# Twelve pieces of w_out's combinations: due times for their stores, other steps and other staging places

## The chip, the cores and the metric

One core of one Trainium2 chip runs the whole program. The metric is the device time of one execution in microseconds (us), as the median over runs. The profile is one further execution of the same program, taken with the hardware profiler.

## The reference

The program computes windowed attention followed by a feed-forward layer with squared ReLU, all in float32:

```python
scores = scale * np.matmul(q, k.transpose(0, 1, 3, 2))      # batch 8, 8 heads, 576 positions, head size 64
mask = (rel >= 0) & (rel < 64)                               # rel = query position - key position
attn = softmax(where(mask, scores, -1e9));  attn_out = attn @ v
x = attn_out.transpose(0, 2, 1, 3).reshape(4608, 512)
h = x @ w_in                                                 # 512 x 2048
out = (np.maximum(h, 0.0) ** 2) @ w_out                      # 2048 x 512
```

Only the last product matters for the change: some of `w_out` is not used as it stands, but as sums and differences of its blocks.

## The kernel before

The 4608 tokens are cut in 12 tiles of 384. Every float32 operand of a product is split into a high and a low part, and a product is three matmuls. The first four tiles go the plain way. The other eight are done in four rounds of two tiles, and each round is eight steps, so there are **steps 0 to 31**. A step s belongs to pair p = s mod 8 of 128-column blocks of `w_in`.

In each step TensorE (PE) first makes seven products with combinations of `w_in` (line 932, 7 x 6 matmuls, function `product`), in the manner of Strassen. Their sums leave PSUM by VectorE (DVE, line 949) and ScalarE (ACT). Then PE does the second layer for the step two back (line 1023, function `second`, 3 x 12 matmuls). From step 26 on the second layer is done with combinations of `w_out` (line 1164, function `fast`). In between come the sections of attention of later tiles: scores, softmax, a transposition (line 276) that needs the weights which GpSimd (POOL) has scaled (line 272), and the product with v (line 298).

Before a round starts, its seven operands are made from the two tiles' attention results (function `operands`). Three subtractions (line 884) run on POOL, the first two into the slab `t`; after them ACT rounds (line 895) and DVE takes the rest (line 896). The operands overwrite those of the round before. Rounds begin at steps 0, 8, 16 and 24.

The combinations of `w_out` that steps 26 and later use are made beforehand by `mixing2` (line 1043), in twelve pieces: six pairs p = 0 to 5, each in two halves c. One piece is six POOL instructions (two additions, line 1051, and four subtractions, line 1055), a rounding on ACT (line 1062), a subtraction on DVE (line 1064) and two stores to the DRAM tensor `mixed2` (line 1067; the trace calls this tensor `mixed`, too). The half c = 0 is made in steps 10 to 15 and c = 1 in steps 18 to 23, a pair per step. A piece needs a **staging place** in SBUF: even pairs use the slab `t`, odd pairs the last quarter of the two slabs `gb0` and `gb1` (key "m2"). In `gb` the low part is written over the place in which POOL builds the sums, so the next piece there can begin on POOL only when the second store has been read out. Slab `t` has three separate parts, and it is also the scratch of `operands`.

The order of instructions on each engine comes from a planner (class `Plan`). Every instruction is recorded with an engine, a cost, the keys it reads and writes, and, for transfers, a landing time. `in_order` gives each a latest start, counted back from the PE instruction that needs it (`late[n]`), and then lists the instructions by simulated time, taking among the ready ones the one with the earliest latest start. A store is needed only by what reads the keys it wrote, so without such a reader nearby its latest start is far off. This order is all that the planner gives: each engine runs its list in order, waiting on semaphores where data or space is missing. All transfers are issued by SyncE (SP) from one such list.

Of the kernel before, what the change touches and what calls it, by code (L numbers as in the profile page):

```python
# [8 lines left out]
F32 = mybir.dt.float32  # L9
# [20 lines left out]
def window_attention_relu2_ffn(ctx: ExitStack, tc: tile.TileContext, q, k, v, w_in, w_out, out):  # L30
    nc = tc.nc
    pe, dve, act, pool, sp = nc.tensor, nc.vector, nc.scalar, nc.gpsimd, nc.sync
    B, H, S, D = q.shape
    NT, DM = out.shape
# [19 lines left out]
    raw_t = att.tile([P, 2, 2, S], F32, name="raw")  # L54
# [306 lines left out]
    def slab(name, dtype, words=4 * DM):  # L361
        if name not in slabs:
            slabs[name] = wpool.tile([P, words], dtype, name="w")
        return slabs[name]
# [62 lines left out]
    def in_turn(x):  # L427
        return x.rearrange("p (a b) -> p b a", a=2)
# [32 lines left out]
    E = mybir.EngineType  # L461
# [55 lines left out]
    mixed2 = dram.tile([NF // 2, P, 4, 2, DM // 2], F32, name="mixed2")  # L517
# [29 lines left out]
    with tc.manual_schedule(engines={E.PE, E.DVE, E.Activation, E.Pool, E.SP}):  # L547
        for token in order.split():
            op, eng = token[0], token[-1] if token[-1] in "dap" else None
            n = int(token[1:].rstrip("dap"))  # L550
# [92 lines left out]
    NP = NF // 2  # L643
# [74 lines left out]
    plan = Plan()  # L718

    def by(op, *args):  # L720
        return lambda: op(*args)
# [3 lines left out]
    wi_n, wo_n, wi, wo = [0], [0], {}, {}  # L725

    def wi_fetch(name, source, keys=()):
        n = wi_n[0]
        wi_n[0] += 1
        slot = n % NWI  # L730
        wi[name] = slot
        plan("sp", 0.45, lambda: sp.dma_start(wi_slot(slot).bitcast(F32), source), keys, [("wi", slot)], 3.5,
             freed(wi_home(slot)[0]) if n < NWI else [], 0.7)
# [16 lines left out]
    def wo_keys(slots):  # L750
        return [("wo", slot, m) for slot in slots for m in range(2)]
# [4 lines left out]
    def block(f, half):  # L756
        return kept[f, :, 0, :, half * 2 * P:(half + 1) * 2 * P]
# [160 lines left out]
    def product(s, n):  # L918
        p = s % NP
        kind = (0, "A11", 2, 3, "A12", "A22", 1)[n]  # L920
        source = mixed[p, :, kind] if isinstance(kind, int) else block(2 * p + (kind[1] == "2"), int(kind[2]) - 1)
        wi_fetch((s, n), source, [("mixed", p, c) for c in range(2)] if isinstance(kind, int) else [])
        slot = wi[s, n]
        if n < 4:
            sums_of[s, n] = bank()
        ps, key = sums_of[s, (0, 1, 2, 3, 1, 2, 3)[n]]

        def do():
            w, x, m = wi_slot(slot), operand(n), 0
            for kk in range(2):  # L930
                for part, xx in ((0, 0), (0, 1), (1, 0)):
                    pe.matmul(ps[:, :TT], lhsT=w[:, part, kk * P:(kk + 1) * P], rhs=in_turn(x[:, xx, kk]),  # L932
                              start=n < 4 and m == 0, stop=m == 5, skip_group_check=True)
                    m += 1
        plan("pe", 0.98, do, [("xo", n, 0), ("xo", n, 1), ("wi", slot)], [key, ("tick", s, n)])
        b, a, c, d = (sums_of.get((s, m), (None, None)) for m in range(4))
        sc, v, u = by(short, 0), lambda: r_t[:, s % 2], by(short, 1 + s % 2)
        kv, ku = ("r", s % 2), ("u", s % 2)
        g11, g21 = ((lambda m=m: g_first(s)[:, m], g_first_keys(s, m)) for m in range(2))
        g12, g22 = ((lambda m=m: g_last(s % 4)[:, m], [("gb", s % 4, m)]) for m in range(2))  # L940
        first_a = [("ghi", m) for m in range(3)] + [("glo", m) for m in range(2)] if s < 3 else []
        if LAST <= s < LAST + 4:
            first_a = [("XF", s % 4 // 2, m, r) for m in range(2) for r in range(SPT)]
        squares = SQUARES if s < LAST else LAST_SQUARES
        first_b = freed(f"gb{s % 4 // 2}") if s < 4 else []
        first_s = freed("part1", "t") if s < 2 else []

        def add(to, keys, ps, kps, other, ko, after=()):
            plan("dve", 0.6, lambda: dve.tensor_tensor(to(), ps, other(), ALU.add), [kps, ko], keys, 0, after)  # L949

        def square(g, pre, where):
            x, keys = g
            if where == "dve":
                plan("dve", 0.57, lambda: dve.scalar_tensor_tensor(x(), x(), 0.0, x(), ALU.max, ALU.mult), [], keys)
                return
            if not pre:
                plan("act", 0.5, lambda: act.activation(x(), x(), AF.Relu), [], keys)
            if where == "act":
                plan("act", 0.5, lambda: act.activation(x(), x(), AF.Square), [], keys)
            else:  # L960
                plan("pool", 0.95, lambda: pool.tensor_tensor(x(), x(), x(), ALU.mult), [], keys)  # L961
        if n == 0:
            plan("act", 0.5, lambda: act.copy(sc(), b[0][:, :TT]), [b[1]], ["sc"], 0, first_s)
        elif n == 1:
            add(v, [kv], a[0][:, :TT], a[1], sc, "sc")
        elif n == 2:
            add(u, [ku], c[0][:, :TT], c[1], v, kv, first_s)
        elif n == 3:
            add(lambda: by_half(g22[0]()), g22[1], ordered(d[0][:, :TT]), d[1], lambda: ordered(u()), ku, first_b)
            square(g22, False, squares[0])  # L970
        elif n == 4:
            plan("act", 0.5, lambda: act.activation(by_half(g11[0]()), ordered(a[0][:, :TT]), AF.Relu), [a[1]], g11[1], 0, first_a)  # L972
            square(g11, True, squares[1])
        elif n == 5:
            add(lambda: by_half(g21[0]()), g21[1], ordered(c[0][:, :TT]), c[1], lambda: ordered(v()), kv, first_a)
            square(g21, False, squares[2])
        elif n == 6:
            add(lambda: by_half(g12[0]()), g12[1], ordered(d[0][:, :TT]), d[1], lambda: ordered(v()), kv, first_b)
            square(g12, False, squares[3])
# [55 lines left out]

    def staging(n):
        x, y = (slab(f"gb{m}", F32)[:, 3 * DM:] for m in range(2))
        z = slab("t", F32)  # L1040
        return [z[:, m * DM:(m + 1) * DM] for m in range(3)] if n else [x, y, x]

    def mixing2(op, s, p, c):
        at = lambda m, dtype=F32: staging(1 - p % 2)[m].bitcast(dtype).rearrange("p (f l c) -> p f l c", f=2, l=2)
        mine = ["m2"] if p % 2 else [("T", 0), ("T", 1)]

        def whole(f):
            slot = wo[(s - 2) // NP, 2 * p + f]
            hi, lo = (wo_slot(slot)[:, part].bitcast(F32).rearrange("p (l c) -> p l c", l=2)[:, :, c * P:(c + 1) * P]
                      for part in range(2))  # L1050
            pool.tensor_tensor(at(0)[:, f], hi, lo, ALU.add)

        def less(to, a, b):
            x = at(0)
            pool.tensor_tensor(x[:, to[0], to[1]], x[:, a[0], a[1]], x[:, b[0], b[1]], ALU.subtract)
        if op == "A":
            for f in range(2):
                plan("pool", 0.81, by(whole, f), wo_keys([wo[(s - 2) // NP, 2 * p + f]]) + [("tick", s, 0)], mine)
            for to, a, b in (((0, 0), (0, 1), (0, 0)), ((0, 1), (1, 1), (0, 1)), ((1, 1), (1, 1), (0, 0)), ((1, 0), (1, 1), (1, 0))):
                plan("pool", 0.54, by(less, to, a, b), [], mine)  # L1060
        elif op == "C":
            plan("act", 0.62, lambda: act.copy(at(1, F32R), at(0)), [("tick", s, 6)], mine)
        elif op == "E":
            plan("dve", 0.7, lambda: dve.tensor_tensor(at(2, F32R), at(0), at(1), ALU.subtract), [("tock", s, 0)], mine)
        else:
            for part in range(2):
                plan("sp", 0.5, lambda part=part: sp.dma_start(
                    mixed2[p, :, :, part, c * P:(c + 1) * P], at(1 + part).rearrange("p f l c -> p (f l) c")),
                     mine + [("tick", s + 1, 1)], [("mixed2", p, c, part)], 4.5, (), 0.9)

    FAST = ("A11", 0, 0), ("A12", 1, 0), ("A22", 2, None), ("S1", 0, None), ("S2", 3, None), ("S4", 1, 1), ("S3", 1, None)

# [140 lines left out]
    for n in range(2 * NF + LAG, NPLAIN * NF):  # L1213
        m = n - 2 * NF
# [14 lines left out]
    marks = {}  # L1229
    for j in range(FULL):  # L1230
        for r in range(2 * SPT):
            i = SPT * NPLAIN + 2 * SPT * (j + 1) + r
            m = 16 * j + (2 * r if r else -4)
            m, n = (0, (1, 4)) if m == 2 else (m, m + 1)
            marks.setdefault(m, []).append(by(burst, i, i - 1))
            marks.setdefault(n, []).append(by(cross, i))
    for c in range(2):
        for p in range(NP - 2):
            s = NP * (c + 1) + 2 + p
            for op, at in ("A", (s, 0)), ("C", (s, 6)), ("E", (s, 7)), ("F", (s + 1, 1)):  # L1240
                marks.setdefault(at, []).append(by(mixing2, op, s, p, c))
    operands(0)
    for s in range(NP * FULL + 2):
        if s < NP * FULL:
            for mark in marks.get(2 * s, []):
                mark()
            for n in range(7):
# [3 lines left out]
                if s < LAST and s % 2 == 0 and n % 2 == 0 or s == FAST_END + 1 and n % 2 == 0:  # L1251
                    f = s // 2 * 2 % NP * 2 + n // 2
# [61 lines left out]
```

## Time and profile before

| what | us |
|---|---|
| median of 3 runs | 869.51 (868.71 to 870.89) |
| the profiled execution itself | 869.36 |
| its span, first to last instruction | 867.6 |
| TensorE busy | 835.3 (96%) |
| VectorE busy | 627.6 (72%) |
| ScalarE busy | 435.6 (50%) |
| GpSimd busy | 244.8 (28%) |

A busy share is an average over the span. TensorE is the engine that is nearly always busy, so time is lost where it stands still or where its granted clock is below 1.00; the other engines count where TensorE waits for them. The mean granted clock is 0.986.

### The profile page before, as it was taken

The page shows a single profiled execution, that of the slowest core. Times are in us where ns is not written, and L with a number is a line of the kernel's source. Part 1 is how long each engine was busy: PE and PEld are TensorE (multiplying, and loading weights), DVE is VectorE, ACT ScalarE, POOL GpSimd, SP SyncE. Part 2 cuts the span into 40 slices and gives each one's busy share as a digit, 9 for nine tenths or more (in the row PEclk, how much of TensorE's full clock was granted, in tenths as well). Part 3 has the DMA queues.
Part 4 walks back from the last instruction along what each step waited for, and adds up shares of the span by engine and source line. Part 5 has one row for each costly group of instructions (what it writes and reads, how often), then busy time and mean ns, then how long its engine had stood idle before and what let it go on. Part 6 is the DMA issues. An engine that isn't in the chain of part 4 may idle for free. (4 is left out here: it accounts for less than half of the span.)

```text
span 867.6 us, 18267 instructions
## 1 busy us (share of the span) xinstructions
PE 835.3 (96%) x6916; PEld 770.1 (89%) x6916; DVE 627.6 (72%) x905; ACT 435.6 (50%) x1178; POOL 244.8 (28%) x314
## 2 busy tenths in 40 slices
PE   7899999999999999999999999796999998999998
PEld 6788988989999999999999999695999997999997
DVE  4999995566667767777786766576666669566876
ACT  5887764645456555554343455242355424455341
POOL 1220003114647501212312431425233534112121
PEclk9899999999999999999999999997999999999999
DMA  9989946646698885988978778796875864698851
GB/s 228 221 252 339 322 204 117 104 107 196 143 229 249 202 170 160 309 195 232 214 255 252 189 194 256 211 230 196 266 234 158 260 214 132 207 304 279 256 170 73
DMA packets 292120, 184.99 MB, mean 213 GB/s; under 512 B 191168, under 2 KB 257216, under 8 KB 289984
## 3 DMA queue, kind: packets, MB, share of 16 engines
q1 hardware_dynamic: 292032, 183.81, 75.4%
q8 instruction: 55, 0.90, 0.5%
q14 instruction: 33, 0.27, 0.1%
HBM read 142.87 MB, written 40.89 MB: 212 GB/s over the span
## 5 line engine op out<-in xcount | busy, mean ns | idle before, releaser
L1023 PE MATMUL banks<-w 128*128 128x512 f32 x888 | 201.5, 383 | 0.0
L1023 PEld LDWEIGHTS banks<-w 128*128 128x128 f32 x888 | 167.1, 190 | 22.1
L404 PE MATMUL banks<-x,w 128*128 128x384 f32 x768 | 138.4, 330 | 2.0 <-ACT r L413 1.9
L446 PE MATMUL banks<-w,g 128*128 128x512 f32 x576 | 136.4, 382 | 0.1
L404 PEld LDWEIGHTS banks<-x,w 128*128 128x128 f32 x768 | 127.1, 190 | 6.8 <-ACT r L413 3.5
L932 PE MATMUL banks<-x,w 128*128 128x384 f32 x768 | 131.0, 327 | 0.3 <-DVE r L949 0.3
L932 PEld LDWEIGHTS banks<-x,w 128*128 128x128 f32 x768 | 126.3, 190 | 0.7 <-DVE r L949 0.6
L446 PEld LDWEIGHTS banks<-w,g 128*128 128x128 f32 x576 | 106.2, 189 | 14.1 <-DVE g L423 0.9
L932 PE MATMUL banks<-w 128*128 128x384 f32 x576 | 105.8, 339 | 11.7 <-DVE w L896 6.8
L932 PEld LDWEIGHTS banks<-w 128*128 128x128 f32 x576 | 97.2, 195 | 14.4 <-DVE w L896 7.6
L263 ACT ACTIVATE sel<-sel,nm 128x64 f32<-128x64 f32 x272 | 90.8, 336 | 23.1 <-DVE nm L257 22.8
L961 POOL TENSOR_TENSOR g<-g 128x384 f32<-128x384 f32 x48 | 44.1, 922 | 206.7 <-ACT g L972 198.7
L1031 DVE TENSOR_TENSOR w<-w,banks 128x512 f32<-128x512 f32 x60 | 40.9, 686 | 41.9 <-PE banks L1023 40.7
L413 ACT ACTIVATE r<-banks 128x384 f32<-128x384 f32 x64 | 31.4, 490 | 72.0 <-PE banks L404 69.3
L272 POOL TENSOR_TENSOR sel<-sel,nm 128x512 f32<-128x512 f32 x33 | 35.9, 1089 | 84.9 <-DVE nm L269 45.6
L536 POOL TENSOR_TENSOR a<-w 128x256 f32<-128x256 f32 x28 | 25.0, 908 | 99.5 <-DVE w L132 73.8
L263 ACT ACTIVATION_READ_ACCUMULATOR sel<-sel,nm 128x1 f32 x272 | 51.2, 188 | 0.0
L1013 ACT CAST w<-w 128x512 fp32r<-128x512 f32 x37 | 23.0, 620 | 55.1 <-PE banks L1023 55.1
L423 DVE TENSOR_TENSOR g<-r,g 128x384 fp32r<-128x384 f32 x64 | 36.7, 577 | 17.8 <-ACT g L421 11.9
L949 DVE TENSOR_TENSOR w<-banks,r 128x384 f32<-128x384 f32 x64 | 38.2, 597 | 13.9 <-PE banks L932 13.6
L280 DVE TENSOR_TENSOR pt<-banks,masks 128x1024 f32<-128x1024 f32 x33 | 40.2, 1219 | 9.9 <-PE banks L276 9.9
L418 DVE TENSOR_TENSOR r<-r 128x384 f32<-128x384 f32 x38 | 24.9, 655 | 27.5 <-ACT r L413 27.4
(163 smaller groups left out, 1282.8 us busy)
## 6 DMA issues: line engine op xcount, KB each, us to landing
w<-mixed SPq DMA_DIRECT2D x128, 256.0 KB, 5.6
w<-kept SPq DMA_DIRECT2D x114, 256.0 KB, 6.1
w<-kept SPq DMA_DIRECT2D x52, 512.0 KB, 7.4
kept<-w SPq DMA_DIRECT2D x16, 1024.0 KB, 7.6
vt<-in_v_dram SPq DMA_DIRECT2D x144, 64.0 KB, 3.3
w<-in_moe_w_in_dram SPq DMA_DIRECT2D x16, 512.0 KB, 7.4
w<-in_moe_w_out_dram SPq DMA_DIRECT2D x16, 512.0 KB, 8.5
raw<-in_q_dram SPq DMA_DIRECT2D x112, 72.0 KB, 3.1
```

The lines of the kernel that those rows point to most:

```text
L263: act.activation(sels[i][:, w, hd], sels[i][:, w, hd], AF.Exp, bias=nms[i][:, n], scale=SCALE, accum_out=sums[i][:, n])
L272: (dve if eng == "d" else pool).tensor_tensor(p, p, rs[i][:, :, None].broadcast_to([P, SW * 2, QB]), ALU.mult)
L280: dve.tensor_tensor(pts[i].rearrange("p (w n) q -> p w n q", n=2), ps_t[i][:, :, None, :].broadcast_to([P, SW, 2, P]), masks.rearrange("p ...
L404: pe.matmul(h_ps, lhsT=weights(kk, part), rhs=in_turn(x[xx][:, kk // 2, kk % 2]), start=n == 0, stop=n == 3 * NK - 1)
L413: act.activation(by_half(rg[n]), ordered(hs.pop(n)), AF.Relu)
L423: (pool if eng == "p" else dve).tensor_tensor(gs[n][1], rg.pop(n), gs[n][0].bitcast(F32), ALU.subtract)
L446: pe.matmul(acc(t, tb), lhsT=gg[:, ts], rhs=in_turn(weights(part)), start=f == 0 and n == 0, stop=f == NF - 1 and n == 2)
L932: pe.matmul(ps[:, :TT], lhsT=w[:, part, kk * P:(kk + 1) * P], rhs=in_turn(x[:, xx, kk]), start=n < 4 and m == 0, stop=m == 5, skip_group_c ...
L949: plan("dve", 0.6, lambda: dve.tensor_tensor(to(), ps, other(), ALU.add), [kps, ko], keys, 0, after)
L961: plan("pool", 0.95, lambda: pool.tensor_tensor(x(), x(), x(), ALU.mult), [], keys)
L1023: pe.matmul(ps, lhsT=gg[:, m // 2, m % 2], rhs=in_turn(wo_slot(w[m])[:, part]), start=m == 0 and n == 0, stop=m == 3 and n == 2)
L1031: plan("dve", 0.72, lambda: dve.tensor_tensor(by_half(parts(tb)), by_half(parts(tb)), ordered(ps), ALU.add), [key], [kp])
```

## The change

It does three things:

- The third product of a step s (n == 2) now "reads" the two stores of the piece of step s - 2. This adds no wait on the chip, it is a key of the planner: the stores must stand in the list ahead of that PE instruction, and their latest start is counted back from it.
- The pieces stand in a table, PIECES (step, pair, half, home). Pair 4's pieces move: from step 14 to step 7 (now its half c = 1), and step 22 now makes its half c = 0. The other ten keep their steps.
- There are new homes: pair 4 in step 7 uses `gb`, pair 4 in step 22 uses the first half of the tile `raw`, pair 5 in step 23 uses its second half. `raw` held q and k of attention, the last of which is read in step 17.

```diff
+        due = [("stored", s - 2, part) for part in range(2)] if n == 2 else []
-        plan("pe", 0.98, do, [("xo", n, 0), ("xo", n, 1), ("wi", slot)], [key, ("tick", s, n)])
+        plan("pe", 0.98, do, [("xo", n, 0), ("xo", n, 1), ("wi", slot)] + due, [key, ("tick", s, n)])
...
-    def staging(n):
-        x, y = (slab(f"gb{m}", F32)[:, 3 * DM:] for m in range(2))
-        z = slab("t", F32)
-        return [z[:, m * DM:(m + 1) * DM] for m in range(3)] if n else [x, y, x]
+    def staging(home):
+        if home == "t":
+            x = slab("t", F32)
+            return [x[:, m * DM:(m + 1) * DM] for m in range(3)]
+        if home == "gb":
+            x, y = (slab(f"gb{m}", F32)[:, 3 * DM:] for m in range(2))
+        else:
+            n = home == "raw1"
+            x, y = (raw_t.rearrange("p a b c -> p (a b c)")[:, (2 * n + m) * DM:(2 * n + m + 1) * DM] for m in range(2))
+        return [x, y, x]
+    STAGED = {"t": [("T", 0), ("T", 1)], "gb": ["m2"], "raw0": ["m3"], "raw1": ["m4"]}
+    PIECES = ((7, 4, 1, "gb"), (10, 0, 0, "t"), (11, 1, 0, "gb"), (12, 2, 0, "t"), (13, 3, 0, "gb"), (15, 5, 0, "gb"),
+              (18, 0, 1, "t"), (19, 1, 1, "gb"), (20, 2, 1, "t"), (21, 3, 1, "gb"), (22, 4, 0, "raw0"), (23, 5, 1, "raw1"))
...
-        mine = ["m2"] if p % 2 else [("T", 0), ("T", 1)]
+        mine = STAGED[home]
...
-                     mine + [("tick", s + 1, 1)], [("mixed2", p, c, part)], 4.5, (), 0.9)
+                     mine + [("tick", s + 1, 1)], [("mixed2", p, c, part), ("stored", s, part)], 4.5, (), 0.9)
```

The diff does not show how the lists move. PE's list is the same row for row. Three places on the other engines follow. Line 1051 becomes 1063, 1055 becomes 1067, 1067 becomes 1079, 961 becomes 962; `w_3681` and `w_3887` are the staging in `gb`, `w_2911` is `t`, `a_1988` holds the attention results.

**SP, steps 13 and 14** (loads of `w_in`'s combinations, line 732, and blocks of `w_out`, line 743), before:

```order
L732 DMA w_3198<-mixed_113 128x512 x2
L732 DMA w_2956<-kept_112 128x2x256
L743 DMA w_3677<-kept_112 128x1024
L732 DMA w_2992<-mixed_113 128x512
L743 DMA w_3677<-kept_112 128x1024
L732 DMA w_3173<-mixed_113 128x512
L743 DMA w_3696<-kept_112 128x1024
L732 DMA w_3272<-kept_112 128x2x256
L1067 DMA mixed2_114<-w_3887 512x1x128
L732 DMA w_3298<-kept_112 128x2x256
L743 DMA w_3696<-kept_112 128x1024
L1067 DMA mixed2_114<-w_3681 512x1x128
```

and with the change:

```order
L157 DMA vt_77<-in_v_dram 64x4x64 x4
L1079 DMA mixed2_114<-w_3887 512x1x128
L1079 DMA mixed2_114<-w_3681 512x1x128
L732 DMA w_3198<-mixed_113 128x512 x2
L732 DMA w_2956<-kept_112 128x2x256
```

The two stores of step 11's piece have moved from behind nine and eleven loads to the front of them. The pair of step 10 moves in the same way ahead of the seven loads of its stretch.

**POOL, steps 15 and 16**, where the second round ends, before:

```order
L961 TENSOR_TENSOR g_3704<-g_3704 128x384 x3
L1051 TENSOR_TENSOR w_3681<-w_3696 128x256 x2
L1055 TENSOR_TENSOR w_3681<-w_3681 128x128
L884 TENSOR_TENSOR w_2911<-a_1988 128x768
L1055 TENSOR_TENSOR w_3681<-w_3681 128x128
L884 TENSOR_TENSOR w_2911<-a_1988,w_2911 128x768
L884 TENSOR_TENSOR a_1988<-a_1988 128x768
```

and with the change, from step 13 on:

```order
L1063 TENSOR_TENSOR w_3681<-w_3930 128x256 x2
L1067 TENSOR_TENSOR w_3681<-w_3681 128x128 x4
L272 TENSOR_TENSOR sel_79<-sel_79,nm_81 128x512
L962 TENSOR_TENSOR g_3704<-g_3704 128x384 x2
L884 TENSOR_TENSOR w_2911<-a_1988 128x768
L884 TENSOR_TENSOR w_2911<-a_1988,w_2911 128x768
L884 TENSOR_TENSOR a_1988<-a_1988 128x768
L962 TENSOR_TENSOR g_3704<-g_3704 128x384
L272 TENSOR_TENSOR sel_79<-sel_79,nm_81 128x512
L962 TENSOR_TENSOR g_3704<-g_3704 128x384
L1063 TENSOR_TENSOR w_3681<-w_3696 128x256 x2
L1067 TENSOR_TENSOR w_3681<-w_3681 128x128 x4
```

The three subtractions of `operands` (line 884) now stand right behind step 13's piece, ahead of step 15's piece; the piece of step 14 (into `w_2911`) is gone from between.

**POOL, steps 22 to 24**, before:

```order
L1051 TENSOR_TENSOR w_2911<-w_3677 128x256 x2
L1055 TENSOR_TENSOR w_2911<-w_2911 128x128 x4
L961 TENSOR_TENSOR g_3704<-g_3704 128x384 x2
L1051 TENSOR_TENSOR w_3681<-w_3696 128x256 x2
L1055 TENSOR_TENSOR w_3681<-w_3681 128x128 x4
L961 TENSOR_TENSOR g_3704<-g_3704 128x384 x2
L884 TENSOR_TENSOR w_2911<-a_1988 128x768
L884 TENSOR_TENSOR w_2911<-a_1988,w_2911 128x768
L884 TENSOR_TENSOR a_1988<-a_1988 128x768
```

and with the change:

```order
L884 TENSOR_TENSOR w_2911<-a_1988 128x768
L1063 TENSOR_TENSOR raw_76<-w_3677 128x256
L884 TENSOR_TENSOR w_2911<-a_1988,w_2911 128x768
L1063 TENSOR_TENSOR raw_76<-w_3677 128x256
L884 TENSOR_TENSOR a_1988<-a_1988 128x768
L1067 TENSOR_TENSOR raw_76<-raw_76 128x128
L962 TENSOR_TENSOR g_3704<-g_3704 128x384
L1067 TENSOR_TENSOR raw_76<-raw_76 128x128
```

The subtractions have moved from behind both last pieces and four squares (line 961) to the place where step 22's piece began.

## Rows read from the trace of the kernel before

**Rows 1.** Stretches: PE alone; us, PE busy (instructions), granted clock, DMA share, GB/s

```profile
402.46:434.65 32.19, 32.19 (x242) 1.00 0.93 226
434.65:465.85 31.20, 31.20 (x229) 1.00 0.84 279
534.05:573.44 39.39, 34.78 (x243) 0.96 0.89 261
573.44:615.92 42.48, 34.75 (x237) 0.88 0.81 218
729.81:750.33 20.52, 16.55 (x80) 0.92 0.45 141
750.33:764.92 14.59, 14.59 (x79) 1.00 0.83 275
```

**Rows 2.** Timeline of PE, steps 12 to 24: start, us, instruction [idle before it]

```profile
520.03 4.06 PE L932 MATMUL banks<-x,w 128*128 128x384 f32 x24
...
537.08 4.06 PE L932 MATMUL banks<-x,w 128*128 128x384 f32 x24
...
550.34 0.66 PE L276 MATMUL banks<-ident,sel 128*128 128x128 f32 x4 [4.01 <-POOL sel L272]
...
593.06 0.69 PE L932 MATMUL banks<-w 128*128 128x384 f32 x1 [4.86 <-ACT w L895]
596.62 5.81 PE L932 MATMUL banks<-w 128*128 128x384 f32 x17 [2.87 <-DVE w L896]
...
734.11 4.45 PE L932 MATMUL banks<-w 128*128 128x384 f32 x17 [3.97 <-DVE w L896]
```

**Rows 3.** Timeline of POOL, steps 13 and 14

```profile
546.69 1.40 POOL L1051 TENSOR_TENSOR w<-w 128x256 f32<-128x256 f32 x2 [20.48 <-DMA vt<-in_v_dram]
...
549.24 1.04 POOL L272 TENSOR_TENSOR sel<-sel,nm 128x512 f32<-128x512 f32 x1
...
554.21 2.51 POOL L1055 TENSOR_TENSOR w<-w 128x128 f32<-128x128 f32 x4
```

**Rows 4.** Timeline of SP, steps 12 to 15: loads and stores as they were issued

```profile
514.23 1.01 SPq L732 DMA_DIRECT2D w<-mixed  x2
...
518.08 1.34 SPq L1067 DMA_DIRECT2D mixed<-w  x2
...
530.15 1.02 SPq L732 DMA_DIRECT2D w<-mixed  x2
...
538.91 0.56 SPq L1067 DMA_DIRECT2D mixed<-w  x1
...
582.51 0.53 SPq L1067 DMA_DIRECT2D mixed<-w  x1
```

**Rows 5.** All 24 stores of line 1067: time from issue to landing

```profile
DMA to landing us min/median/max: 2.7/6.1/7.8
```

**Rows 6.** Timeline of POOL, steps 15 and 16

```profile
585.35 1.42 POOL L1051 TENSOR_TENSOR w<-w 128x256 f32<-128x256 f32 x2 [3.62 <-DMA mixed<-w]
...
588.17 1.80 POOL L884 TENSOR_TENSOR w<-a 128x768 f32<-128x768 f32 x1 [0.54 <-DMA mixed<-w]
```

**Rows 7.** Timeline of POOL, steps 22 and 23

```profile
712.11 1.43 POOL L1051 TENSOR_TENSOR w<-w 128x256 f32<-128x256 f32 x2 [3.32 <-DMA mixed<-w]
...
720.86 0.84 POOL L961 TENSOR_TENSOR g<-g 128x384 f32<-128x384 f32 x1 [4.82 <-ACT g L972]
...
723.43 2.54 POOL L884 TENSOR_TENSOR w<-a 128x768 f32<-128x768 f32 x1
```

**Rows 8.** Timeline of POOL, step 6: the subtractions ahead of the round of step 8

```profile
420.38 1.82 POOL L884 TENSOR_TENSOR w<-a 128x768 f32<-128x768 f32 x1 [9.57 <-ACT a L313]
```

**Rows 9.** Landing of the load issued at 514.23 (line 732)

```profile
DMA to landing us min/median/max: 4.1/4.1/4.1
```

**Rows 10.** Timeline of DVE, step 23: one operation, without and beside POOL's subtractions

```profile
720.45 0.56 DVE L954 SCALAR_TENSOR_TENSOR w<-w 128x384 f32<-128x384 f32 x1
...
724.21 2.18 DVE L954 SCALAR_TENSOR_TENSOR w<-w 128x384 f32<-128x384 f32 x1
```

More of the change, by code (lines that the diff above doesn't have):

```diff
@@ L1034, in second, with mixing2 @@
             plan("sp", 0.4, lambda: sp.dma_start(out[row:row + P, :], parts(tb)), [kp], [], 3.0, (), 0.7)
-    def staging(n):
-        x, y = (slab(f"gb{m}", F32)[:, 3 * DM:] for m in range(2))
-        z = slab("t", F32)
-        return [z[:, m * DM:(m + 1) * DM] for m in range(3)] if n else [x, y, x]
-    def mixing2(op, s, p, c):
-        at = lambda m, dtype=F32: staging(1 - p % 2)[m].bitcast(dtype).rearrange("p (f l c) -> p f l c", f=2, l=2)
-        mine = ["m2"] if p % 2 else [("T", 0), ("T", 1)]
+    def staging(home):
[11 more added lines that the diff above has]
+              (18, 0, 1, "t"), (19, 1, 1, "gb"), (20, 2, 1, "t"), (21, 3, 1, "gb"), (22, 4, 0, "raw0"), (23, 5, 1, "raw1"))
+    def mixing2(op, s, p, c, home):
+        at = lambda m, dtype=F32: staging(home)[m].bitcast(dtype).rearrange("p (f l c) -> p f l c", f=2, l=2)
+        mine = STAGED[home]
+        free = [("raw", g, n) for g in range(2) for n in range(8)] if home[:3] == "raw" else []
         def whole(f):
@@ L1057, in mixing2 @@
             for f in range(2):
-                plan("pool", 0.81, by(whole, f), wo_keys([wo[(s - 2) // NP, 2 * p + f]]) + [("tick", s, 0)], mine)
+                plan("pool", 0.81, by(whole, f), wo_keys([wo[(s - 2) // NP, 2 * p + f]]) + [("tick", s, 0)], mine, 0, free)
             for to, a, b in (((0, 0), (0, 1), (0, 0)), ((0, 1), (1, 1), (0, 1)), ((1, 1), (1, 1), (0, 0)), ((1, 0), (1, 1), (1, 0))):
@@ L1236, in window_attention_relu2_ffn @@
             marks.setdefault(n, []).append(by(cross, i))
[L1237 to L1241, printed above, removed]
+    for s, *piece in PIECES:
+        for op, at in ("A", (s, 0)), ("C", (s, 6)), ("E", (s, 7)), ("F", (s + 1, 1)):
+            marks.setdefault(at, []).append(by(mixing2, op, s, *piece))
     operands(0)
```

## The prediction

> **What bounds the kernel.** I read the page first: TensorE (PE) is busy 835.3 of 867.6 us, so nothing pays but what lets PE stand still or slows its clock. Then I cut PE's time by steps and set each stretch against one of the same make-up [rows 1]. The attention sections repeat with a period of eight steps, so steps 13 and 14 should take as long as 5 and 6, and steps 15 and 16 as long as 7 and 8. They do not: 39.39 us against 32.19, and 42.48 against 31.20. Step 24 takes 20.52, the next step, with the same instructions, 14.59. The stretches that serve as measure have PE busy throughout at a granted clock of 1.00; the three long ones have gaps, and clocks of 0.96, 0.88 and 0.92. So the excess is 7.20 + 11.28 + 5.93 = **24.4 us**. It holds the gaps and the slower matmuls right after them: in the gap's wake 17 matmuls of line 932 took 5.81 us, at a clock that in that stretch is a mixture of 1.2 and 2.4 GHz.
>
> Who ends the gaps stands on PE's timeline [rows 2]: at 550.34 the transposition had waited 4.01 us for POOL's scaling (line 272); at 593.06 and 596.62 step 16's first product waited 4.86 and 2.87 us for the roundings and remainders of the operands; at 734.11 step 24's did so for 3.97 us. I followed each back.
>
> Gap at 550. POOL's scaling is queued behind step 13's piece, whose first addition stood still for 20.48 us, to 546.69 [rows 3]. The row names a load of v as releaser. I take it to be the store instead: the piece goes to `gb`, which step 11's piece had used, and that piece's second store was issued at 538.91 [rows 4]; 546.69 is 7.8 us later, the longest landing of any of these stores [rows 5]. The load of v is merely the last thing that landed before.
>
> Gap at 593. Step 15's piece on POOL began at 585.35, when the second store of step 13's piece, issued at 582.51 [rows 4], had let `gb` go. The first subtraction of the operands came at 588.17, released by a store of step 14's piece, which lies in `t`, where the subtraction writes [rows 6]. Both wait for stores that stand late in SP's list.
>
> Gap at 734. Here no store holds the subtractions directly. Step 23's piece began at 712.11, after a store again, then come two squares that wait for PE's step, and the subtractions only at 723.43 [rows 7]. They wait for their place in the list.
>
> How it should look is shown by the round of step 8, ahead of which there are no pieces: the first subtraction ran at 420.38, as soon as ACT had delivered the attention result [rows 8], and steps 7 and 8 lost nothing [rows 1].
>
> **The change, part by part.** Arithmetic is the same: twelve pieces, 24 stores, PE's list untouched. So every term is a matter of place and of waiting.
>
> *Step 13's piece.* Step 11's stores now stand ahead of the load that was issued at 530.15 [rows 4]. They are issued at about 530.15 and 530.8; with the longest landing, 7.8 us, `gb` is free at 538.6. Two additions take 1.40 us, four subtractions 2.51, the scaling 1.04 [rows 3]: ready at 543.6. PE asks for it at 550.34 - 4.01 = 546.3 [rows 2]. That leaves 2.7 us, so the gap goes, with its slow wake: all 7.20 us of steps 13 and 14, as nothing else was in them. If the landing took 3 us more than any seen, a part would remain.
>
> *Operands of step 16.* With pair 4 gone from step 14, the last user of `t` is step 12's piece, whose stores stand where they stood, at about 547. The subtractions stand ahead of step 15's piece and wait only for step 14's attention result. In step 6 that came at 420.38 [rows 8], 14.3 us before step 7 began at 434.65 [rows 1]. At 1.8 us [rows 8] to 2.5 us [rows 7] each the three are done 6.7 us or more before step 15 begins, and only after the products of step 15 may the old operands be overwritten. What is left to ACT and DVE is what they did in step 7 [rows 1, 8]. So steps 15 and 16 should take what 7 and 8 take: 11.28 us. Step 15's piece follows on POOL when step 13's stores, now as a pair ahead of five loads, have long landed.
>
> *Operands of step 24.* The subtractions stand where step 22's piece stood and start with step 22's attention result. Step 23 began some 14.6 us before 729.81, at 715.2; 14.3 us earlier is 700.9, so they come 22 us sooner than 723.43 [rows 7]. The pieces in `raw` wait for no store. They are interleaved, so the last subtraction ends about two additions later. Again the place is that of step 6: 5.93 us.
>
> *Pair 4 in step 7.* Six POOL instructions, 3.9 us, in a stretch in which POOL is mostly idle: nothing on the path. Its remainder on DVE lies between step 8's sums; 0.7 us there, and PE's banks are asked for again only three products later: nothing. Without that cover it would cost 0.7.
>
> *What SP now does first.* This is the price. A pair of stores takes 1.34 us to issue [rows 4] and then shares the transfer engines with the loads behind it. The tightest case is step 12's seventh product: its load was issued at 514.23 [rows 4] and landed 4.1 us later [rows 9], at 518.3. The row at 520.03 is step 12's products four to seven, 24 matmuls in 4.06 us [rows 2], so the seventh is due three quarters on, at 523.1. Behind step 10's stores the load is issued at 515.6; if it then lands as slowly as the slowest store, 7.8 us, that is 523.4, 0.3 late; at 4.1 us it has 3.4 to spare. For step 13's seventh product (537.08 + 3.05 = 540.1) the load moves from 530.15 to 531.5, and 7.8 us later is 539.3. So the cost lies between 0 and about 2 us for the two places together, if a slow wake is added; I take 0, since both loads are nearer to the row of 4.1. None of PE's gaps in these rows was ended by a load [rows 2]; I take the later loads to have more room.
>
> *Who may be late next.* In step 22 DVE's remainder of pair 4 stands ahead of an addition, and ACT's rounding before it waits for POOL. I keep 1 us for such waits, which the old gaps cover now.
>
> *The subtractions beside VectorE.* One DVE operation took 0.56 us alone and 2.18 beside POOL's subtractions [rows 10]. They now run beside step 14's and step 22's sums. The row of step 6 shows such a neighbourhood without loss for PE, so I cost it at nothing. The Trainium skill ("SBUF — State Buffer", section "Who interferes with whom") has a rule that speaks against the change here: a VectorE instruction with two SBUF inputs and a GpSimd instruction that reads SBUF shut each other out for a whole instruction. The trace agrees with its 2.18 us. By that rule alone, with all of it on the path, the sum would be that of rival 2.
>
> Sum: 869.36 - 24.4 + 1 = 846.0. The profiled execution is 0.15 below the median, which changes nothing at this size. **846 us.**
>
> **Rivals.**
> 1. *The loads pay, or the store lands later than any before.* The stretch from 512 to 546 is where transfers crowd, so stores in front may hold both tight loads, or leave a rest of the gap at 550. Price: up to half of the first term, 3.6, and 2 for the loads: 846 to 852. For it: 0.3 us of margin in the worst case. Against it: the rows' usual landings.
> 2. *VectorE is held up by the moved subtractions.* Three subtractions, each lengthening one DVE operation by 2.18 - 0.56 = 1.6 us [rows 10], at two rounds: 9.7 us, if all of it is on the path: 846 + 9.7 = 855.7. Against it: step 6.
> 3. *The change doesn't do what it says.* If SP is late for another cause than its order (transfers full, issue slots taken), or the 20.48 us wait was for the load of v after all, stores come no sooner and the gaps stay: 869, no change. Against it: issue at 538.91 plus 7.8 is 546.7, when POOL went on, to the tenth.
> 4. *Slower: SP's list as the new bound.* Nine of the twelve pairs now stand ahead of loads they were behind. Each can delay those loads by 1.34 us of issue and 7.8 - 4.1 = 3.7 of landing, some 5 us. As soon as six pairs or more have that on PE's path, it is over 24.4 + 2.6: six give 846 + 30 = 876. Against it: it needs loads that run less than 9 us ahead at six places, and I found that lead (514.23 to 523.1) at one.
>
> **How the numbers follow.** A difference under 0.3% (2.6 us) can't be told from none here. Forecast 0.74; rival 1 0.13, rival 2 0.06 (both faster); rival 3 0.04; rival 4 0.03. So faster 0.93, same 0.04, slower 0.03. The range reaches from 842.5, where the whole excess goes and some small waits with it, to 854, which takes in rival 1 and part of rival 2.
>
> **What would show it.** Right: on PE's timeline no wait on line 272 near step 13, none on lines 895 and 896 at steps 16 and 24; those three stretches 32, 31 and 14.6 us long at a clock of 1.00; the subtractions of line 884 starting right after ACT's copy of the attention result; POOL's longest wait for a store of line 1079 a few us. Wrong: PE waiting for a load into line 932 (rivals 1 and 4), or for sums of DVE that grew beside line 884 (rival 2); POOL still standing at line 1063 for many us (rival 3).

## The result and the profile after

The changed kernel takes **845.21 us** (median of 6 runs, 844.53 to 846.79) against 869.94 (867.88 to 871.45) for the kernel before in the same session: ratio 0.9721, interval 0.9704 to 0.9738. A later repetition (846.71 against 871.14) is told with the experiments. The profiled execution took 844.53 us, 24.8 less than that of before; its span is 842.8.

The page: PE's busy time fell too, from 835.3 to 827.0 us, since slowed matmuls count as busy: the 80 of step 24 took 16.55 us of PE's time at a clock of 0.92 [rows 1], and take 14.60 below. In the clock row only one slice, near the start, is below 9.

```profile
PE 827.0 (98%) x6916; PEld 763.5 (91%) x6916; DVE 621.8 (74%) x905; ACT 435.4 (52%) x1178; POOL 243.6 (29%) x314
...
PEclk9899999999999999999999999999999999999999
```

The view that decides is PE's time in the stretches of [rows 1]: steps 5 and 6, 7 and 8, 13 and 14, 15 and 16, then step 24 and step 25.

```profile
401.74:433.93 32.19, 32.19 (x243) 1.00 0.92 232
433.93:465.13 31.20, 31.20 (x229) 1.00 0.85 265
533.61:565.90 32.29, 32.29 (x242) 1.00 1.00 294
565.90:597.01 31.11, 31.11 (x237) 1.00 1.01 268
710.90:725.50 14.60, 14.60 (x80) 1.00 0.67 198
725.50:740.09 14.59, 14.59 (x79) 1.00 0.84 274
```

The three long stretches now are as long as those of the same make-up, PE busy throughout at a granted clock of 1.00. Before they were 39.39, 42.48 and 20.52. They gave back 7.10 + 11.37 + 5.92 = 24.39 of the 24.8 us. PE's longest waits are these; none is at line 932, and the 0.9 us on line 272 is elsewhere in the program.

```profile
PE banks L298 <- DVE pt L280: 2.2, 3, 1.6
PE banks L404 <- ACT r L413: 2.0, 4, 0.6
PE banks L512 <- POOL ident masks.py:199: 1.5, 1, 1.5
...
PE banks L276 <- POOL sel L272: 0.9, 1, 0.9
```

PE's timeline, against [rows 2]: the transposition that had waited 4.01 us starts without a wait, and so do the first products of steps 16 and 24. The first row, step 12's products four to seven, is for the loads below.

```profile
519.59 4.06 PE L932 MATMUL banks<-x,w 128*128 128x384 f32 x24
...
545.72 0.60 PE L276 MATMUL banks<-ident,sel 128*128 128x128 f32 x4
...
580.49 3.09 PE L932 MATMUL banks<-w 128*128 128x384 f32 x18
...
710.90 3.09 PE L932 MATMUL banks<-w 128*128 128x384 f32 x18
```

POOL's timeline, against [rows 3, 6, 7, 8]: the piece of step 7, that of step 13 with the scaling behind it, the subtractions for step 16, step 15's piece, and the first subtraction for step 24.

```profile
428.90 1.86 POOL L1063 TENSOR_TENSOR w<-w 128x256 f32<-128x256 f32 x2
...
533.62 1.42 POOL L1063 TENSOR_TENSOR w<-w 128x256 f32<-128x256 f32 x2 [7.86 <-DMA mixed<-w]
...
539.33 1.04 POOL L272 TENSOR_TENSOR sel<-sel,nm 128x512 f32<-128x512 f32 x1 [2.28 <-ACT g L973]
...
551.56 1.84 POOL L884 TENSOR_TENSOR w<-a 128x768 f32<-128x768 f32 x1 [9.61 <-ACT a L313]
...
562.68 1.42 POOL L1063 TENSOR_TENSOR w<-w 128x256 f32<-128x256 f32 x2 [1.15 <-DMA mixed<-w]
...
682.41 1.82 POOL L884 TENSOR_TENSOR w<-a 128x768 f32<-128x768 f32 x1 [8.74 <-ACT a L313]
```

Step 13's piece starts at 533.62 instead of 546.69 and now names a store as its releaser. Both sets of subtractions are released by ACT's copy of the attention result, as in step 6 [rows 8], 14.3 and 13.9 us before PE begins the next step (565.90, and 696.31 on PE's timeline).

SP's timeline, against [rows 4]: the pairs of steps 10 and 11, each ahead of the load it used to follow.

```profile
514.50 1.24 SPq L1079 DMA_DIRECT2D mixed<-w  x2
515.84 1.19 SPq L732 DMA_DIRECT2D w<-mixed  x2
...
529.77 1.24 SPq L1079 DMA_DIRECT2D mixed<-w  x2
531.10 1.26 SPq L732 DMA_DIRECT2D w<-mixed  x2
```

All 24 stores took from issue to landing, against 2.7/6.1/7.8 before [rows 5]:

```profile
DMA to landing us min/median/max: 2.6/4.7/7.3
```

### The profile page after: what moved, and what is told of

Its sections match the earlier page's. It is cut to its first block, busy times and chain, and to the rows that moved or that the text cites. A ratio compares the mean times of both kernels' runs of the same rounds, so it can differ in the third digit from the quotient of the medians.

```text
span 842.8 us, 18259 instructions
## 1 busy us (share of the span) xinstructions
PE 827.0 (98%) x6916; PEld 763.5 (91%) x6916; DVE 621.8 (74%) x905; ACT 435.4 (52%) x1178; POOL 243.6 (29%) x314
## 4 chain that ended last, share of the span: by engine, by line
PE 86%; DVE 6%; SPq 3%; ACT 2%; issue 1%; DMA 1%; POOL 0%; DVEq 0%; ACTq 0%; POOLq 0%
PE banks L932 26%; PE banks L1024 24%; PE banks L446 11%; PE banks L404 11%; PE banks L1176 5%; PE banks L235 4%; PE banks L298 4%; PE banks L276 2%; DVE a L123 1%; SPq L157 1%; SPq L147 1%; SPq L185 1%; DVE w L132 1%; DVE a L125 1%; ACT a L118 1%
## 5 line engine op out<-in xcount | busy, mean ns | idle before, releaser
L1024 PEld LDWEIGHTS banks<-w 128*128 128x128 f32 x888 | 165.9, 189 | 21.6
L932 PE MATMUL banks<-w 128*128 128x384 f32 x576 | 100.7, 329 | 0.0
L932 PEld LDWEIGHTS banks<-w 128*128 128x128 f32 x576 | 93.4, 189 | 1.6
```

The lines of the kernel that those rows point to most:

```text
L1024: pe.matmul(ps, lhsT=gg[:, m // 2, m % 2], rhs=in_turn(wo_slot(w[m])[:, part]), start=m == 0 and n == 0, stop=m == 3 and n == 2)
```

## The experiments

All are edits of the kernel before or of the changed kernel. The kernel before took 870.88 us (868.35 to 875.11) beside experiments 1 to 4, 871.14 (869.4 to 872.8) beside 5 to 8, and 870.32 (867.29 to 872.58) beside 9. So the changed kernel's ratio of 0.972 is the mark for each ratio.

### 1. A due time for one piece: is the first gap step 11's store?

The kernel before, with a due time for the stores of step 11's piece alone.

```diff
+        due = [("stored", s - 2, part) for part in range(2)] if n == 2 and s == 13 else []
-        plan("pe", 0.98, do, [("xo", n, 0), ("xo", n, 1), ("wi", slot)], [key, ("tick", s, n)])
+        plan("pe", 0.98, do, [("xo", n, 0), ("xo", n, 1), ("wi", slot)] + due, [key, ("tick", s, n)])
...
-                     mine + [("tick", s + 1, 1)], [("mixed2", p, c, part)], 4.5, (), 0.9)
+                     mine + [("tick", s + 1, 1)], [("mixed2", p, c, part), ("stored", s, part)], 4.5, (), 0.9)
```

> The kernel before with a due time for one pair of stores alone, that of step 11's piece. On SP only these two stores move, ahead of the load that was issued at 530.15; on POOL step 13's piece stays ahead of the scaling of line 272. Theory (POOL stood 20.48 us for this store): the wait of line 276 at 550 goes, steps 13 and 14 take 32.2 instead of 39.4 us, the gaps at steps 16 and 24 stay: 869.9 - 7.2 = 862.7, within 1.5. Rival (POOL stood for the load of v that the row names): nothing moves, 869 to 871.

Measured: 867.93 us (862.7 to 870.15, 10 runs), ratio 0.9955 (0.9933 to 0.9978). The mechanism held and the size did not. Steps 13 and 14, then 15 and 16, in this run:

```profile
535.77:568.06 32.29, 32.29 (x243) 1.00 0.99 286
568.06:614.57 46.51, 33.76 (x237) 0.85 0.83 221
```

Besides the two stores some loads of this part of SP's list, one rounding on ACT and two squares on POOL change places; POOL keeps step 13's piece ahead of the scaling. The first gap is gone, 39.39 to 32.29, so the 20.48 us wait of [rows 3] was for the store and not for the load of v that the row names. But the next stretch grew from 42.48 to 46.51. PE's timeline at step 16:

```profile
592.70 0.69 PE L932 MATMUL banks<-w 128*128 128x384 f32 x1 [9.88 <-ACT w L895]
596.26 4.88 PE L932 MATMUL banks<-w 128*128 128x384 f32 x17 [2.87 <-DVE w L896]
```

PE now arrives at 592.70 - 9.88 = 582.82, and before at 593.06 - 4.86 = 588.20 [rows 2]: 5.4 us sooner. The operands come only 0.4 sooner. Why, POOL's and SP's timelines show:

```profile
587.81 1.80 POOL L884 TENSOR_TENSOR w<-a 128x768 f32<-128x768 f32 x1 [1.29 <-DMA mixed<-w]
```

```profile
581.33 0.50 SPq L147 DMA_DIRECT2D raw<-in_k_dram  x1
...
583.21 1.21 SPq L1068 DMA_DIRECT2D mixed<-w  x2
```

The pair that frees `t` stands behind sixteen loads of `raw` and goes out at 583.21 (583.79 before), though PE comes so much sooner; the subtraction follows at 587.81 (588.17 before, [rows 6]). What holds those loads to the same time is not shown; from 556 to 583 the DMA engines are busy for 0.98 of the time in this run, and were for 0.86 before. So the first gap had covered part of the second: 7.1 us came back, 4.0 went again, 3.1 stayed.

### 2. Due times for all stores, without the table

The kernel before with the condition of the change; the other lines as in experiment 1.

```diff
+        due = [("stored", s - 2, part) for part in range(2)] if n == 2 else []
```

> The due times for all twelve pieces, pieces and places as before (pair 4 in step 14 in t, in step 22 in t, pair 5 in step 23 in gb). Theory (the due time cures only the first gap, since step 14's stores keep their place behind the loads of raw and the subtractions keep their place behind step 15's and step 23's pieces): 7.2 us less at steps 13 and 14, at steps 15 and 16 at most 2 of 11.3 us less, step 24 as before: 860 to 863. Rival (late stores are the whole cause, and the due times alone cure it): 845 to 848.

Measured: 866.07 us (864.13 to 867.77, 5 runs), ratio 0.9923 (0.9898 to 0.9948). Neither number: some 3 us above the theory's range, 18 above the rival's. At step 16 PE still waits 8.66 and 2.61 us, at step 24 3.97, for the same lines as before. Steps 13 and 14, then 15 and 16:

```profile
536.12:568.41 32.29, 32.29 (x242) 1.00 0.99 295
568.41:614.25 45.84, 34.56 (x237) 0.85 0.84 225
```

As the theory had it, due times by themselves do not repair the second and third gap. It had expected steps 15 and 16 to gain up to 2 us; they lose 3.4 (45.84 against 42.48), as in experiment 1.

### 3. The table without the due times

```diff
-        due = [("stored", s - 2, part) for part in range(2)] if n == 2 else []
+        due = []
```

> The changed kernel without the due times: steps and places from the new table, stores as late as the planner likes. Theory: the first gap is back (step 11's stores again stand behind the loads of step 14), 7.2 us; the other two stay away, because t is free and the subtractions keep their early place on POOL: 845.2 + 7.2 = 852.4, within 2. Rival (the table matters only through the due times): 860 or more.

Measured: 856.62 us (852.88 to 858.9, 4 runs), ratio 0.982 (0.9784 to 0.9856). That is 2.2 us above the theory's range and below the rival's 860. The profiled execution, 852.88, is the shortest of the four, and it lies in the theory's range. In it steps 13 and 14 take 39.20 us, 15 and 16 31.77, step 24 14.60: one gap is back, the other two stay away. PE's timeline, then POOL's:

```profile
550.55 1.11 PE L276 MATMUL banks<-ident,sel 128*128 128x128 f32 x4 [3.98 <-POOL sel L272]
```

```profile
546.90 1.40 POOL L1063 TENSOR_TENSOR w<-w 128x256 f32<-128x256 f32 x2 [20.44 <-DMA mixed<-w]
```

Here the row names the store itself. With experiment 2, the table is thus what removes the gaps of steps 16 and 24, the due times that of step 13. By the medians the due times are worth more than the 7.1 us of that stretch (856.62 here against 846.71 in experiment 5); the other executions were not profiled, and where their 3 to 6 us over the profiled one lie stays open.

### 4. Steps 22 and 23 in their old homes

```diff
-              (18, 0, 1, "t"), (19, 1, 1, "gb"), (20, 2, 1, "t"), (21, 3, 1, "gb"), (22, 4, 0, "raw0"), (23, 5, 1, "raw1"))
+              (18, 0, 1, "t"), (19, 1, 1, "gb"), (20, 2, 1, "t"), (21, 3, 1, "gb"), (22, 4, 0, "t"), (23, 5, 1, "gb"))
```

> The changed kernel with step 22's piece in t and step 23's in gb again, as before the change. Due times and step 7 stay. On POOL the three subtractions go back behind both pieces and the four squares. Theory (the gap at step 24 is their place in POOL's list): step 24 takes 20.5 us instead of 14.6 and all else is as with the change: 845.2 + 5.9 = 851.1, within 1.5. Rival (the gap came from step 23's piece waiting for a late store in gb, which the due times cure): 845 to 847.

Measured: 853.69 us (852.95 to 853.87, 4 runs), ratio 0.9789 (0.9765 to 0.9813). The theory held in the cause; the time is 1 us above its range. PE's timeline at step 24, which takes 21.77 us (712.97 to 734.74):

```profile
717.27 5.81 PE L932 MATMUL banks<-w 128*128 128x384 f32 x17 [3.97 <-DVE w L896]
```

and POOL's:

```profile
692.12 1.52 POOL L1063 TENSOR_TENSOR w<-w 128x256 f32<-128x256 f32 x2 [0.17 <-DMA mixed<-w]
...
706.59 2.54 POOL L884 TENSOR_TENSOR w<-a 128x768 f32<-128x768 f32 x1
```

Here a store delays step 23's piece by 0.17 us only, instead of the 3.32 of [rows 7]. The subtractions still come last, and the gap has its full 3.97 us. Their place in POOL's list is the cause there, not a landing.

### 5. The changed kernel again

> The changed kernel itself, on the same chip as the next three, as their measure: 845.2 within 1.5, ratio to the kernel before 0.972.

Measured: 846.71 us (846.54 to 847.22, 4 runs), ratio 0.9723 (0.9705 to 0.9741). In each 100 us of its profile from 200 to 800 PE is busy for 100.00 us at a granted clock of 1.00.

### 6. Pair 4 back in step 14

```diff
-    PIECES = ((7, 4, 1, "gb"), (10, 0, 0, "t"), (11, 1, 0, "gb"), (12, 2, 0, "t"), (13, 3, 0, "gb"), (15, 5, 0, "gb"),
+    PIECES = ((10, 0, 0, "t"), (11, 1, 0, "gb"), (12, 2, 0, "t"), (13, 3, 0, "gb"), (14, 4, 1, "t"), (15, 5, 0, "gb"),
```

> The changed kernel with pair 4's second half made in step 14 in t again instead of in step 7 in gb. Due times and raw stay. On SP that piece's stores stand behind the 16 loads of raw again, on POOL the subtractions stand behind step 15's piece. The two runs with due times alone showed that these loads end at about 581 whether or not the first gap is there, because the transfers fill that stretch. Theory (step 14's stores in t hold the subtractions, and the first gap covered part of that): stretch of steps 15 and 16 some 45 to 47 us instead of 31.2, no other gap: 859 to 862. Rival (the terms add up as in the prediction's sum): 845.2 + 11.3 = 856.5.

Measured: 861.4 us (856.85 to 863.03, 4 runs), ratio 0.9882 (0.9848 to 0.9916). The median is the theory's, the profiled execution (856.85, the shortest) that of the rival. In it steps 15 and 16 take 42.49 us, 11.4 more than in the changed kernel and less than the theory's 45 to 47, and there is no other gap. The loads of `raw`, which the theory had ending at about 581, end at 578.3 in this execution, and step 14's stores go out at 578.93. PE's and POOL's timelines:

```profile
587.95 0.69 PE L932 MATMUL banks<-w 128*128 128x384 f32 x1 [6.36 <-ACT w L895]
591.25 4.64 PE L932 MATMUL banks<-w 128*128 128x384 f32 x17 [2.62 <-DVE w L896]
```

```profile
583.35 1.80 POOL L884 TENSOR_TENSOR w<-a 128x768 f32<-128x768 f32 x1 [8.22 <-DMA mixed<-w]
```

So the place and the releaser are shown: a piece in `t` in step 14 makes the subtractions wait for its stores. The size varies by 6 us between executions, where the kernel before varies by 3.4 beside it. That would fit a wait whose end is set by a crowd of transfers, but only the shortest execution was profiled, so where the others lose more is not shown.

### 7. Every store twice: how much room has SP?

The changed kernel with a second, spare DRAM tensor that nobody reads; each store goes there first and then to its place.

```diff
...
-                plan("sp", 0.5, lambda part=part: sp.dma_start(
-                    mixed2[p, :, :, part, c * P:(c + 1) * P], at(1 + part).rearrange("p f l c -> p (f l) c")),
+                plan("sp", 0.5, lambda part=part: [sp.dma_start(
+                    to[p, :, :, part, c * P:(c + 1) * P], at(1 + part).rearrange("p f l c -> p (f l) c"))
+                    for to in (spare2, mixed2)],
```

> The changed kernel with each of the 24 stores issued twice, first into a spare tensor of the same shape: twice the issue time on SP (1.2 us more a pair) and 6.3 MB more to move, in the same places. Theory (the loads behind the stores have lead to spare, 6.8 us at the tightest product, in step 12): PE waits for loads of line 932 at one to three places, 845 to 852. Rival (SP's list is the new bound, and the gain hangs on a few spare us): 5 us at each of the nine moved pairs and more, 870 and up.

Measured: 855.26 us (850.78 to 856.27, 4 runs), ratio 0.9808 (0.9771 to 0.9846), so 8.5 us over experiment 5. PE waits for transfers at four places on its timeline:

```profile
536.21 0.33 PE L298 MATMUL banks<-pt,vt 64*64 64x64 f32 x4 [0.39 <-DMA vt<-in_v_dram]
...
543.16 1.21 PE L933 MATMUL banks<-x,w 128*128 128x384 f32 x6 [0.56 <-DMA w<-mixed]
...
562.04 1.21 PE L933 MATMUL banks<-x,w 128*128 128x384 f32 x6 [1.50 <-DMA w<-mixed]
...
594.88 1.21 PE L933 MATMUL banks<-x,w 128*128 128x384 f32 x6 [2.61 <-DMA w<-mixed]
```

The last three are the seventh products of steps 13, 14 and 16; step 12's, the tightest by the prediction, does not wait. The rival of the long list, 870 and more, is far off, but the room that the changed kernel leaves its loads is smaller than the theory had it: doubling 24 stores costs 8.5 us, more than the theory allowed. The run adds issue time on SP and bytes at once, and does not tell which of the two made the loads late.

### 8. A deadline one step earlier

```diff
-        due = [("stored", s - 2, part) for part in range(2)] if n == 2 else []
+        due = [("stored", s - 1, part) for part in range(2)] if n == 2 else []
```

> The changed kernel with the due times one step on instead of two. Eight pairs of stores move further ahead on SP, and the loads of raw with them ahead of several loads of line 732; POOL keeps its order but for squares. Theory (no store holds anything up any more, so earlier stores buy nothing, and SP has spare time in most places): 845 to 849. Rival (a store due so early meets an unfinished remainder of VectorE and holds SP's list): PE waits for loads of line 932 at several places, 855 and more.

Measured: 861.74 us (861.48 to 862.56, 4 runs), ratio 0.9896 (0.9877 to 0.9915). The size is the rival's; the mechanism is neither's, for PE waits for no load of `w_in`. It waits 10.4 us, eight times, for sums of line 950, as here on its timeline:

```profile
564.14 3.71 PE L932 MATMUL banks<-x,w 128*128 128x384 f32 x12 [3.14 <-DVE w L950]
```

and DVE's timeline shows why:

```profile
563.25 0.17 DVE L266 TENSOR_SCALAR nm<-nm 128x8 f32<-128x8 f32 x1 [2.83 <-ACT sel L263]
563.46 0.20 DVE L269 RECIPROCAL nm<-nm 128x8 f32<-128x8 f32 x1
563.58 0.51 DVE L950 TENSOR_TENSOR w<-banks,r 128x384 f32<-128x384 f32 x1
```

Two short instructions of the softmax, which wait for ACT's exponentials, now stand ahead of the sums that free PE's banks. So it is at seven of the eight places, 10.2 of the 10.4 us; the eighth, 0.18 us, stands among remainders of line 896. My new theory: `due` is a key that the product reads, so in the planner's simulated time that product also *waits* for the store's modelled landing. One step on, the store has not landed there. The plan's PE runs late, the softmax seems to be ready first, and DVE's list is written for a PE that on the chip is not late.

### 9. The same deadline, without the plan's waiting

The latest start is still counted back from the product, but the product no longer waits for the store in the simulated time.

```diff
...
+            must = [list(x) for x in after]
+            for n, x in self.due.items():
+                for m in x:
+                    must[m].append(n)
             for n in reversed(range(len(ops))):
                 if ops[n][0] != "pe":
-                    late[n] = min([late[m] for m in after[n]], default=clock) - sum(ops[n][m] for m in (1, 4, 5)) - HOP
+                    late[n] = min([late[m] for m in must[n]], default=clock) - sum(ops[n][m] for m in (1, 4, 5)) - HOP
...
-        plan("pe", 0.98, do, [("xo", n, 0), ("xo", n, 1), ("wi", slot)] + due, [key, ("tick", s, n)])
+        plan("pe", 0.98, do, [("xo", n, 0), ("xo", n, 1), ("wi", slot)], [key, ("tick", s, n)])
+        plan.due[len(plan.ops) - 1] = [plan.wrote[k] for k in due if k in plan.wrote]
```

> This is the run with a deadline one step on, with one thing taken out of the planner: the product that sets the deadline no longer waits in the plan's clock for the store's modelled landing; the deadline alone is kept. The stores stand as early in SP's list as in that run (step 11's and step 15's pairs three loads sooner than in the changed kernel), and DVE's softmax sums (lines 266 and 269) go back to where the changed kernel has them. If the 15 us of the run with one step came from the plan's late PE, which moved the softmax sums ahead of the sums of line 950, this comes to 845 to 848, and PE's waits on line 950 are gone. Rival: the earlier stores themselves, or other moves of that order (line 896's remainders, the sums of line 1015), cost it: then 855 or more, and PE waits at the same places.

Measured: 847.36 us (844.86 to 848.07, 4 runs), ratio 0.9731 (0.9709 to 0.9753). The theory held: the 14 us are gone, PE waits for no sum of that line, and from 200 to 800 us it is busy for 100.00 us in each 100. On DVE's timeline the softmax sum is again behind the sums, here line 955, and waits for nothing:

```profile
558.24 0.64 DVE L955 TENSOR_TENSOR w<-banks,r 128x384 f32<-128x384 f32 x1
...
559.39 0.17 DVE L266 TENSOR_SCALAR nm<-nm 128x8 f32<-128x8 f32 x1
```

All 24 stores have the places in SP's list that they had in experiment 8: six pairs, those of steps 7, 10, 12, 15, 18 and 23, are ahead of loads that they are behind in the changed kernel, and step 11's pair is where it was. So these early stores are harmless; the late PE of the plan was not. With the deadline of two steps this version of the planner gives the very lists of the changed kernel, so there the waiting key changed nothing. A deadline one step earlier gains nothing either, since there is no gap left for it to close.

## Why the prediction was right

**The excess.** 24.4 us were read from stretches of the same make-up, and 24.39 came. The three terms of 7.20, 11.28 and 5.93 came as 7.10, 11.37 and 5.92. The 1 us kept for new small waits was not needed; 846.0 without it is 845.0, against 845.21 measured.

**Step 13's piece.** Right in the cause (experiment 1), too careful in the size. I put the stores at 530.15 and 530.8 and took the longest landing, 7.8 us, for the second. They went out from 529.77 on, the second at 530.4; it landed 3.1 us later, and POOL began at 533.62. The scaling ended at 540.37, and not at 543.6. One reading was off: the 7.8 us that I counted in the kernel before, 538.91 to 546.69, ends when POOL goes on. That store itself had landed after 7.6 us, at 546.5 and so 0.2 us ahead of POOL. The agreement with the longest landing of [rows 5] was chance; the store was the right one all the same, as experiment 1 shows.

**Operands of steps 16 and 24.** Right, place and time: the rows of POOL repeat step 6, 14.3 and 13.9 us ahead against 14.3. I said that step 13's stores would have landed long before step 15's piece; the piece still waited 1.15 us for them, which nobody had to pay for.

**SP's price.** I put the two tight loads at 515.6 and 531.5; they went out at 515.84 and 531.10. The first is due at 519.59 + 3.05 = 522.6, so it had 6.8 us, and before 523.1 - 514.23 = 8.9. They landed 5.3 and 5.7 us after their issue, against 4.1 and 3.8 before, so the first had 1.5 us to spare, and not the 3.4 of the usual landing. PE did not wait. The cost was at the lower end, 0, but it was nearer than I thought, and experiment 7 used up the room at step 13's seventh product, the second of the two, and at two later ones.

**The subtractions beside VectorE (rival 2).** One DVE operation, beside the last subtraction of the round and then alone, on DVE's timeline of the changed kernel:

```profile
555.93 1.57 DVE L955 SCALAR_TENSOR_TENSOR w<-w 128x384 f32<-128x384 f32 x1
...
558.66 0.56 DVE L955 SCALAR_TENSOR_TENSOR w<-w 128x384 f32<-128x384 f32 x1
```

It was stretched by 1.0 us (before 2.18 - 0.56 = 1.6, [rows 10]), and PE, busy for all of that stretch, paid nothing. The rule in the Trainium skill ("SBUF — State Buffer", section "Who interferes with whom") agrees with the stretching; the price of rival 2 needed it on the path, where it was not.

**Pair 4 in step 7.** Six instructions in 1.86 + 2.52 = 4.4 us instead of 3.9, and steps 5 to 8 are as long as before.

**Rivals 1, 3 and 4.** No load held PE (1 and 4); the lists moved as the change says (3), and the store was the cause.

**What the sum hid.** It treats its terms as separable. For the whole change that is harmless, as no gap remains into which one could move. For a part of it, it is wrong: due times alone brought 3 to 5 us (experiments 1 and 2) where the first term says 7.2, and a reader who had costed them by that term would have promised too much by half or more. The other way round it is not shown. By the medians undoing one part alone cost 7.0 (experiment 4 against 5), 9.9 (experiment 3) and 14.7 (experiment 6), in sum 31.6 and not 24.4; but in the profiled executions the stretches concerned grew by 7.2, 6.9 and 11.4, in sum 25.5, and what the other executions lose beyond that was not traced.

## What to carry to other kernels

Set a suspect stretch against one of the same instructions without the disturbance: the difference holds the gap and the slow matmuls after it, and it came out to 0.1 us a term. But such terms add up only if every gap behind is closed too; an early arrival at a wait whose end is set elsewhere is given back there (4.0 of 7.1 us in experiment 1). A due time in a planner should be a deadline only: where it also makes the simulated consumer wait, the lists of engines that have nothing to do with it are written for a delay that does not exist (14 us between experiments 8 and 9).

## What I had not expected of the hardware

A 256 KB store lands in 2.6 to 7.3 us in the changed kernel. The window of step 11's second store in the changed kernel, which takes in the first as well, and that of step 11's second store before:

```profile
DMA to landing us min/median/max: 2.6/2.9/3.1
```

```profile
DMA to landing us min/median/max: 7.6/7.6/7.6
```

Issued ahead of the loads the two took 2.6 and 3.1 us; behind eleven loads the second had taken 7.6. That its place among the loads made this difference is not shown. One store speaks against it: step 13's, issued at 582.51 right behind the loads of `raw` [rows 4], landed after 2.7 us. Nor does the share of the DMA engines in use explain it alone: it was 1.04 while that store was under way, 1.06 while the slow one was, and 0.83 while step 11's two were in the changed kernel.

In steps 13 to 16 of the changed kernel the transfers fill 1.00 of the DMA engines' time, 0.89 and 0.81 before, and PE stands still nowhere in these steps: full DMA engines were no limit there.
